# Part of the first h step's products moved into the attention's visits, and the constant products moved to another PSUM bank

## Chip, cores and metric

One NeuronCore of a Trainium2 chip runs the whole program. The metric is device time in microseconds (us) of one launch. Engines are named as in the profile: PE is the matrix engine (PEld its weight loads), DVE the vector engine, ACT the scalar engine, POOL the GpSimd engine, SP the queue from which nearly all DMAs are issued.

## What is computed

Attention over 8 batches x 8 heads x 576 positions of 64 elements, each query seeing 32 keys (four heads the last 32 positions, four heads every fourth of the last 128), and then a feed-forward layer on its 4608 rows of 512.

```python
def _attn_ref(q, k, v):
    scores = scale * np.matmul(q, k.transpose(0, 1, 3, 2))
    ...
    scores = np.where(masks[None, :, :, :], scores, -1000000000.0)
    scores = scores - np.max(scores, axis=-1, keepdims=True)
    attn = np.exp(scores)
    attn = attn / (np.sum(attn, axis=-1, keepdims=True) + 1e-09)
    return np.matmul(attn, v).astype(np.float32)

def _moe_ref(x, w_in, w_out):
    h = x @ w_in
    sp = np.maximum(h, 0.0) + np.log1p(np.exp(-np.abs(h)))
    g = h * erf(sp)
    return (g @ w_out).astype(np.float32)
```

## The kernel before

The attention is cut into 72 units of 256 queries of one pair of heads (two heads side by side). A unit needs ten pieces of work. PE multiplies queries by keys (`scores`, into the two PSUM banks sp0 and sp1, one for each head; a unit uses 128 of the first 256 columns of each, odd and even units apart). DVE adds the mask and takes the maximum (`mask_max`, line 235): four operations, the first two on sp0, the other two on sp1. ACT takes the exponent and its sum (`exponents`, line 245, four operations and their sums). POOL adds a small number to the sum (line 250). DVE takes the reciprocal (line 257), POOL multiplies (line 258). PE transposes (line 263). The result is copied to the tile pT (line 267). PE multiplies it by the values (`values`, line 282), and ACT copies the result into rows of x (line 324).

The first 14 units are worked off in **visits** 0 to 13 (`first_visit`). Visit n transposes unit n-3, scores unit n, copies the transposed unit n-3 and multiplies it by its values, normalizes unit n-2, masks unit n, copies the rows of unit n-3, and takes the exponent of unit n. The order on every engine is the order in which the code is written; nothing is reordered. In between stand **constant products** of PE (`busy`, line 364): 128x128 by 128x512 in bf16, of ones, into the PSUM bank h, where nobody reads them. They are there so that PE is not idle. There are six after the scores of visits 0 to 2, and in visits 3 to 13 two after the scores and two after the values.

When a row of x is complete (every second visit from the 5th: channels cc = 0 at visit 5, 1 at 7, 2 at 9, 3 at 11), ACT rounds it to its high part (`part_hi`, line 329), and DVE subtracts to get the low part (`part_lo`, line 335), in the visit that follows, or, for cc = 3, at the end of visit 11.

Visits 1 to 9 also prepare weights, which arrive as pairs of integers and are made into high and low parts: a DMA into one of three tiles dbl (line 431, 512 KB), an ACT operation on it in the next visit or later (line 451), three DVE operations in the visit after that (lines 464 to 466; the last of them frees the dbl tile, and the next DMA into it is issued), an ACT cast to the high part (line 446), a DVE subtraction to the low part (line 460). In a visit DVE does line 460 for one block, then 464 to 466 for another; this comes behind `mask_max`. In visits 1 to 9 the copy of line 267 is done by ACT, later by DVE. On ACT the order is: copy of line 267, cast of 446, line 451, row copies, the high part of x, exponents.

Then come the steps x = 0, 1, 2, ... of the feed-forward layer. Step x computes half j = x % 2 of step t = x // 2: `mm1` makes 128 columns of h for 512 tokens, in bank h for j = 0 and in bank tx for j = 1. Twelve products of 128x128 by 128x512 in 32-bit form stand for one matrix product of full precision: for each of four channels cc the pairs high-high, high-low and low-high (line 528). DVE copies the bank out (`take`, line 600). The remaining attention units are interleaved: step x = 0 transposes unit 11, then runs `mm1`, `values` of unit 11 and the scores of unit 14, and the steps 1, 2, ... go on so. The copy of pT and the DVE operations on weights come ahead of `take` in steps 0 to 3. From t = 2 on (x = 4), `mm2` (line 643) multiplies by the second weights.

The framework adds the waits between engines. It keeps two engines apart when they touch the same PSUM bank of one tile, even in different columns.

Of the kernel before, what the change touches and what calls it, by code (L numbers as in the profile page):

```python
# [18 lines left out]
P = 128  # L19
# [8 lines left out]
KEYS = STRIP + WIN  # L28
# [3 lines left out]
CC = DM // P  # L32
FT = DF // P
TOK = 512
# [19 lines left out]
PAIR = 2  # L54
# [14 lines left out]
FREE = FIRST - LAG + 4  # L69

EARLY = 9

SAVED = 2 * (HALF + 1) + 1

# [35 lines left out]
def ends(t):  # L110

    return t + 1 == NT or STEPS[t][2] != STEPS[t + 1][2]
# [19 lines left out]
PARTS = SPU // SIDE  # L132
# [14 lines left out]
def attn_moe_kernel(ctx: ExitStack, tc: tile.TileContext, qk, v, masks, eye, w_in, w_out, out):  # L147
    nc = tc.nc
# [16 lines left out]
    win_at = win.rearrange("p (a j k i c n) -> p a j k i c n", a=SPC, j=PAIR, k=2, i=2, c=2)  # L165
# [14 lines left out]
    spb = [ps.tile([P, TOK], F32, name=f"sp{i}") for i in range(2)]  # L180
    sps = [b[:, 0:2 * PARTS * KEYS].rearrange("p (i b k) -> p i b k", i=2, k=KEYS) for b in spb]
    bank = ps.tile([P, TOK], F32, name="tx")
# [22 lines left out]
    def load_qk(u):  # L205
        if u < NU:
            n = QW + key_start(u, SPU - 1) + KEYS
            nc.sync.dma_start(out=qkz[u % 2][:, 0:n], in_=qk[u, :, 0:n])

    def load_v(u):  # L210
        if has(u):
            nc.sync.dma_start(out=vz[u % 2], in_=v[u].rearrange("p (s h d) -> p s h d", s=SIDE, h=2))
# [3 lines left out]
    twice = CC // 2  # L216

    def scores(u):
        i = u % 2
        for s in range(SPU):  # L220
            at, (p, r) = QW + key_start(u, s), divmod(s, SIDE)
            for h in range(2):
                hs = slice(h * D, (h + 1) * D)
                nc.tensor.matmul(sps[h][r * STRIP:(r + 1) * STRIP, i, p, :], qkz[i][hs, s * STRIP:(s + 1) * STRIP],  # L224
                                 qkz[i][hs, at:at + KEYS], start=True, stop=True,
                                 tile_position=(h * D, r * STRIP))

    def mask_max(u):

        pr = probs[u] = work.tile([P, 2 * PARTS, KEYS], F32, name="prob", bufs=LAG + 1)  # L230
        nmax = maxes[u] = small.tile([P, 2 * PARTS], F32, name="nmax", bufs=LAG + 1)
        for h in range(2):
            for p in range(PARTS):
                g = PARTS * h + p
                nc.vector.tensor_tensor_reduce(  # L235
                    out=pr[:, g, :], in0=sps[h][:, u % 2, p, :], in1=mask[QUADS.index(kinds(u, p))],
                    scale=-SCALE, scalar=HUGE,
                    op0=ALU.add, op1=ALU.min, accum_out=nmax[:, g:g + 1],
                )

    def exponents(u):
        nmax = maxes.pop(u)
        sums[u] = small.tile([P, 2 * PARTS], F32, name="ssum", bufs=LAG + 1)
        for j in range(2 * PARTS):
            nc.scalar.activation(  # L245
                out=probs[u][:, j, :], in_=probs[u][:, j, :], func=AF.Exp,
                scale=-1.0, bias=nmax[:, j:j + 1], accum_out=sums[u][:, j:j + 1],
            )
        if u < FIRST:
            nc.gpsimd.tensor_scalar(sums[u], sums[u], 1.0e-9, None, op0=ALU.add)  # L250

    def normalize(u):
        rinv = small.tile([P, 2 * PARTS], F32, name="rinv")

        if u >= FIRST:
            nc.vector.tensor_scalar(sums[u], sums[u], 1.0e-9, None, op0=ALU.add)  # L256
        nc.vector.reciprocal(out=rinv, in_=sums.pop(u))
        nc.gpsimd.tensor_tensor(probs[u], probs[u], rinv.broadcast_to([P, 2 * PARTS, KEYS]), op=ALU.mult)  # L258

    def transposes(u):  # L260
        pr = probs.pop(u)
        for h in range(2):
            nc.tensor.transpose(out=turn_place(u)[:, h * P:(h + 1) * P],  # L263
                                in_=pr[:, PARTS * h:PARTS * (h + 1), :].rearrange("p a k -> p (a k)"), identity=ident)

    def turned(u, copy):
        copy(out=pz[u in second][:, 0:2 * P], in_=turn_place(u))
# [7 lines left out]
    def values(u):  # L275
        vt, pt = vz[u % 2], pz[u in second]
        for s in range(SIDE):
            qs = slice(s * STRIP, (s + 1) * STRIP)
            for p in range(PARTS):
                ks, xp = slice(p * KEYS, (p + 1) * KEYS), place(u, p)  # L280
                for h in range(2):
                    nc.tensor.matmul(xp[h * D:(h + 1) * D, qs], vt[ks, s, h, :],  # L282
                                     pt[ks, h * P + s * STRIP:h * P + (s + 1) * STRIP], start=True, stop=True,
                                     tile_position=(p * KEYS, h * D))
# [37 lines left out]
    def rows(u):  # L322
        for to, src in rows_of(u):
            nc.scalar.copy(out=to, in_=src)  # L324
# [7 lines left out]
    def part_lo():  # L332
        while halved:
            hi, lo, src = halved.pop(0)
            nc.vector.tensor_tensor(out=lo, in0=src, in1=hi.bitcast(F32), op=ALU.subtract)
# [4 lines left out]
    def finish(u):  # L340

        for it in [i for i in x_rows if PER * (u + 1) >= NBLK * (i + 1)]:
            (b, hp), r = divmod(it, HP), x_rows.pop(it)
            if b == 0:
                part_hi(xs[hp][:, 0, :], xs[hp][:, 1, :], r)
            elif b == 1 and hp < twice:
                part_hi(*(w[:, TAIL:TOK] for w in tails(hp)), r[:, 0:TOK - TAIL])
            elif b == 1:
                whole[hp] = r
            if b:  # L350
                soon(store_x, b, hp, slice(TOK - TAIL if b == 1 else 0, S), r)
# [4 lines left out]
    def has(u):  # L356
        return 0 <= u < NU

    idle = plain.bitcast(BF16)[:, 0:TOK]

    def busy(k):

        for _ in range(k):
            nc.tensor.matmul(h, idle[:, 0:P], idle, start=True, stop=True)  # L364

    def first_visit(n):

        m = n - LAG
        copy = nc.scalar.copy if 1 <= n <= EARLY else nc.vector.tensor_copy
        if has(m):  # L370
            transposes(m)
        scores(n)
        load_qk(n + 2)
        busy(2 if has(m) else 6)
        if has(m):
            turned(m, copy)
        if 1 <= n <= EARLY:
            prep_act()
        if has(m):
            values(m)  # L380
            busy(2)
        if has(n - 2):
            normalize(n - 2)
        mask_max(n)
        part_lo()
        if has(m):
            rows(m)
            finish(m)
        if m == NBLK - 1:
            part_lo()  # L390
        exponents(n)
        load_v(n - 1)
# [6 lines left out]
    for g in range(DF // TOK):  # L399
        for c in range(CC):  # L400
            hi, lo = (win_at[:, 2 * g:2 * g + 2, :, c // 2, i, c % 2, :] for i in range(2))
# [38 lines left out]
    def prep_act():  # L440


        calls[0] += 1
        if made:
            w, hi, lo = made.popleft()
            nc.scalar.copy(out=hi, in_=like(w, hi))
            rest.append((calls[0], w, hi, lo))
        if staged:
            i, d, hi, lo = staged.popleft()
            w = io.tile([P, TOK], F32, name="w", bufs=4)  # L450
            nc.scalar.activation(out=w, in_=d[:, :, 1].bitcast(F32), func=AF.Abs, scale=REBASE)
            begun.append((calls[0], i, d, hi, lo, w))
# [20 lines left out]
    h = ps.tile([P, TOK], F32, name="h")  # L473
# [41 lines left out]
                nc.sync.dma_start(out=src[:, a - c * TOK:a - c * TOK + n], in_=xT[b][cc][:, s0:s0 + n])  # L515
                a += n

    def mm1(t, j):
        c, ftp, _ = STEPS[t]
        hi, lo = at[c]  # L520
        ft = ftp * PAIR + j

        ccs = list(range(CC))
        if ends(t) and j == PAIR - 1:
            ccs = ccs[twice:] + ccs[:twice]
        for k, cc in enumerate(ccs):
            for i, (w, x) in enumerate(((0, hi), (0, lo), (1, hi))):
                nc.tensor.matmul((h, bank)[j], win_at[:, ftp, j, cc // 2, w, cc % 2, :], x[cc],  # L528
                                 start=(k == 0 and i == 0), stop=(k == CC - 1 and i == 2))

    ws = dram.tile([SPC, P, len(LEFT) * KIND], F32, name="ws")
    sums_of = {}
# [223 lines left out]
    for k in range(1, DOUBLES):  # L756
        i = 2 * SPC * k
# [13 lines left out]
    i = 2 * SPC * FIN  # L771
# [4 lines left out]
    for p in (1, 2, 3):  # L776
        j = i - 13 + p
# [533 lines left out]
    with tc.manual_schedule():  # L1311
        nc.gpsimd.memset(idle, 1.0)
        busy(8)
        load_qk(0)
        nc.sync.dma_start(out=cst[:, 0:NMASK * KEYS], in_=masks)
        load_qk(1)
        nc.sync.dma_start(out=ident, in_=eye)
        for n in range(FIRST):
            if n < 3:
                load_w(n)  # L1320
            first_visit(n)
            if 1 <= n <= EARLY:
                prep_dve()
# [15 lines left out]
        for x in range(2 * NT):  # L1339
            t, j = divmod(x, 2)  # L1340
# [183 lines left out]
```

## Time and profile before

| what | us |
|---|---|
| median of 3 runs (885.29 to 886.21) | 886.17 |
| span of the profiled execution, first to last instruction | 885.7 |
| PE busy | 864.7 |
| DVE busy | 696.6 |
| ACT busy | 608.8 |
| first score product | 4.82 |
| transposes of unit 11, where step x = 0 begins on PE | 50.72 |
| first product of `mm2` | 72.99 |

The profile gives the span of the profiled execution; the time taken around it is the median less the span, 0.47 us. An instruction's row in the timeline has its start, its duration, its engine and line, what it writes and reads, how many are merged, and in brackets how long the engine was idle before it and who released it. Rows of windows have the busy time of each engine, then the clock that was granted to PE (1.00 is full), and the share of DMA engines that were busy.

### The profile page before, as it was taken

Reading aid. Unit: us, or ns where it says so; the run is one execution under the profiler, and the core shown is the slowest. Engines: PE = TensorE matmul, PEld = TensorE weight load, DVE = VectorE, ACT = ScalarE, POOL = GpSimd, SP = SyncE. Lnnn points to the kernel's source line nnn. Section 1 sums busy time; section 2 is a strip of 40 time slices with the busy share of each in tenths; the row PEclk is TensorE's granted clock in tenths of the full one; section 3 lists DMA queues with packets and bytes.
Section 4 is the critical chain, followed back from the end, with each engine's and each line's share of the span. In section 5 each row is a group of like instructions: output and inputs, shape, how many; then the busy total and the mean of one; then the engine's idle time right before and its main releaser. Section 6 shows DMA issues by size and latency. Waiting matters only on the chain.

```text
span 885.7 us, 21974 instructions
## 1 busy us (share of the span) xinstructions
PE 864.7 (98%) x8410; PEld 710.3 (80%) x8422; DVE 696.6 (79%) x1766; ACT 608.8 (69%) x1364; POOL 79.7 (9%) x97
## 2 busy tenths in 40 slices
PE   7799999999999999999999999999999999999998
PEld 3467888888888888878888888888888788889998
DVE  5878888888688889877766875767886868788994
ACT  6889988897797886675677652774656447784442
POOL 2322200111111100001000000000000000000000
PEclk9899999999999999999999999999999999999999
DMA  8874445464567797666576843674778449999331
GB/s 276 291 235 149 147 158 173 160 238 136 178 213 262 283 327 281 206 215 241 185 236 218 283 177 102 210 234 166 216 248 313 150 144 319 319 345 369 121 131 60
DMA packets 83161, 193.03 MB, mean 218 GB/s; under 512 B 9072, under 2 KB 25712, under 8 KB 79984
## 3 DMA queue, kind: packets, MB, share of 16 engines
q1 hardware_dynamic: 80096, 183.17, 61.0%
q10 hardware_dynamic: 2960, 8.46, 2.4%
q8 instruction: 66, 1.08, 0.5%
q14 instruction: 39, 0.32, 0.1%
HBM read 133.92 MB, written 57.67 MB: 216 GB/s over the span
## 4 chain that ended last, share of the span: by engine, by line
PE 90%; DMA 4%; ACT 2%; DVE 2%; issue 1%; POOL 1%; SPq 0%; DVEq 0%; POOLq 0%; ACTq 0%
PE acc L643 33%; PE h L800 10%; PE tx L800 10%; PE h L528 7%; PE tx L528 7%; PE sp L800 6%; PE sp L282 3%; PE acc L1163 3%; PE sp L224 3%; PE sp L1163 2%; PE sp L263 1%; DMA dbl<-in_w_in_dram 1%; PE tx L1163 1%; DMA win<-wd 1%; PE h L1163 1%; PE h L364 1%
## 5 line engine op out<-in xcount | busy, mean ns | idle before, releaser
L643 PE MATMUL acc<-wout_hi,ghi 128*128 128x512 f32 x448 | 177.7, 397 | 0.5 <-ACT ghi L618 0.5
L643 PE MATMUL acc<-wout_lo,ghi 128*128 128x512 f32 x448 | 174.8, 390 | 0.0
L643 PE MATMUL acc<-wout_hi,glo 128*128 128x512 f32 x448 | 124.1, 390 | 0.7 <-DVE glo L619 0.7
L258 POOL TENSOR_TENSOR prob<-prob,rinv 128x256 f32<-128x256 f32 x72 | 71.6, 1001 | 472.9 <-DVE ssum L256 237.1
L245 ACT ACTIVATE prob<-prob,nmax 128x64 f32<-128x64 f32 x288 | 96.4, 339 | 10.9 <-DVE nmax L235 10.6
L643 PEld LDWEIGHTS acc<-wout_hi,glo 128*128 128x128 f32 x448 | 83.9, 188 | 19.2 <-DVE glo L619 1.4
L643 PEld LDWEIGHTS acc<-wout_hi,ghi 128*128 128x128 f32 x448 | 84.2, 188 | 18.4 <-ACT ghi L618 1.4
L643 PEld LDWEIGHTS acc<-wout_lo,ghi 128*128 128x128 f32 x448 | 84.2, 188 | 16.6
L235 DVE CUSTOM_DVE_ANT_0 prob<-sp,cst 128x64 f32<-128x64 f32 x288 | 45.2, 220 | 36.7 <-ACT rows L324 25.9
L849 ACT ACT_TABLE_LOAD x26 | 33.4, 1283 | 48.6 <-DVE hc L817 24.6
L800 PE MATMUL tx<-win 128*128 128x512 f32 x216 | 55.8, 394 | 0.0
L800 PE MATMUL h<-win 128*128 128x512 f32 x216 | 55.8, 393 | 0.0
L245 ACT ACTIVATION_READ_ACCUMULATOR prob<-prob,nmax 128x1 f32 x288 | 54.9, 191 | 0.0
L528 PE MATMUL h<-x,win 128*128 128x512 f32 x192 | 48.8, 396 | 0.0
L528 PE MATMUL tx<-x,win 128*128 128x512 f32 x192 | 48.0, 392 | 0.0
L800 PEld LDWEIGHTS h<-win 128*128 128x128 f32 x216 | 39.9, 188 | 9.3 <-DVE dbl L819 0.7
L800 PEld LDWEIGHTS tx<-win 128*128 128x128 f32 x216 | 39.9, 188 | 9.1 <-DVE hc L819 0.3
L324 ACT COPY rows<-sp 128x128 f32<-128x128 f32 (+7 forms) x167 | 27.5, 306 | 27.3 <-PE sp L224 26.8
L849 ACT ACTIVATE s<-dbl 128x1024 f32<-128x1024 f32 x22 | 23.3, 1061 | 27.4 <-DVE dbl L817 27.3
L528 PEld LDWEIGHTS h<-x,win 128*128 128x128 f32 x192 | 35.4, 188 | 8.0
L528 PEld LDWEIGHTS tx<-x,win 128*128 128x128 f32 x192 | 35.7, 188 | 7.5
L282 PEld LDWEIGHTS sp<-pT,v 64*64 64x64 f32 x1824 | 29.3, 134 | 10.6 <-DVE s L612 4.6
(338 smaller groups left out, 1942.8 us busy)
## 6 DMA issues: line engine op xcount, KB each, us to landing
win<-ws SPq DMA_DIRECT2D x24, 1024.0 KB, 5.3
v<-in_v_dram SPq DMA_DIRECT2D x72, 256.0 KB, 4.7
win<-ws SPq DMA_DIRECT2D x24, 768.0 KB, 5.9
qk<-in_qk_dram SPq DMA_DIRECT2D x48, 272.0 KB, 5.1
dbl<-in_w_in_dram SPq DMA_DIRECT2D x16, 512.0 KB, 4.3
dbl<-in_w_out_dram SPq DMA_DIRECT2D x16, 512.0 KB, 4.3
ws<-x SPq DMA_DIRECT2D x32, 256.0 KB, 5.0
win<-wd SPq DMA_DIRECT2D x14, 512.0 KB, 8.9
```

The costliest lines, as they stand in the source:

```text
L224: nc.tensor.matmul(sps[h][r * STRIP:(r + 1) * STRIP, i, p, :], qkz[i][hs, s * STRIP:(s + 1) * STRIP], qkz[i][hs, at:at + KEYS], start=True ...
L235: nc.vector.tensor_tensor_reduce(out=pr[:, g, :], in0=sps[h][:, u % 2, p, :], in1=mask[QUADS.index(kinds(u, p))], scale=-SCALE, scalar=HUG ...
L245: nc.scalar.activation(out=probs[u][:, j, :], in_=probs[u][:, j, :], func=AF.Exp, scale=-1.0, bias=nmax[:, j:j + 1], accum_out=sums[u][:, ...
L258: nc.gpsimd.tensor_tensor(probs[u], probs[u], rinv.broadcast_to([P, 2 * PARTS, KEYS]), op=ALU.mult)
L263: nc.tensor.transpose(out=turn_place(u)[:, h * P:(h + 1) * P], in_=pr[:, PARTS * h:PARTS * (h + 1), :].rearrange("p a k -> p (a k)"), iden ...
L282: nc.tensor.matmul(xp[h * D:(h + 1) * D, qs], vt[ks, s, h, :], pt[ks, h * P + s * STRIP:h * P + (s + 1) * STRIP], start=True, stop=True, t ...
L324: nc.scalar.copy(out=to, in_=src)
L528: nc.tensor.matmul((h, bank)[j], win_at[:, ftp, j, cc // 2, w, cc % 2, :], x[cc], start=(k == 0 and i == 0), stop=(k == CC - 1 and i == 2))
L643: nc.tensor.matmul(args["out"], args["lhsT"], args["rhs"], start=args["start"], stop=args["stop"])
L800: nc.tensor.matmul(bank_, w[:, wi, c, :], x[c][:, xi, :], start=(c == 0 and n == 0), stop=(c == 1 and n == 2))
L849: nc.scalar.activation(out=l, in_=e, func=AF.Softplus)
L1163: nc.tensor.matmul(y, x[:, at_], w, start=(q == 0 and j == 0 and n == 0), stop=(q == QUART - 1 and j == 1 and n == 2))
```

## The change

Two things change. First, `mm1` of t = 0 is cut up. A table says which channel and half is done in which visit: channel 0 in visits 7 and 8, channel 1 in 9 and 10, channel 2 in 11 and 12, each with j = 0 first. So 18 of the 24 products of t = 0 stand in visits 7 to 12, between the scores and the values, and one of the two constant products there is dropped. The six products of channel 3 stay at x = 0 and x = 1. Second, since the banks h and tx now hold sums from visit 7 on, the constant products write the free half of bank sp1 (columns 256 to 511), each as two of 256 columns, in all visits from the first.

```diff
+FORMED = {7: [(0, 0)], 8: [(0, 1)], 9: [(1, 0)], 10: [(1, 1)], 11: [(2, 0)], 12: [(2, 1)]}
+LEFT_OVER = [3]
...
     def busy(k):
-        for _ in range(k):
-            nc.tensor.matmul(h, idle[:, 0:P], idle, start=True, stop=True)
+        n = 2 * PARTS * KEYS
+        for _ in range(2 * k):
+            nc.tensor.matmul(spb[1][:, n:TOK], idle[:, 0:P], idle[:, n:TOK], start=True, stop=True)
+
+    def early(n):
+        for cc, j in FORMED.get(n, ()):
+            mm1_part(0, j, [cc])
...
         load_qk(n + 2)
-        busy(2 if has(m) else 6)
+        early(n)
+        busy(2 if has(m) and n not in FORMED else 1 if has(m) else 6)
...
-    def mm1(t, j):
+    def mm1_part(t, j, ccs):
         c, ftp, _ = STEPS[t]
         hi, lo = at[c]
-        ft = ftp * PAIR + j
-        ccs = list(range(CC))
+        order = list(range(CC))
         if ends(t) and j == PAIR - 1:
-            ccs = ccs[twice:] + ccs[:twice]
-        for k, cc in enumerate(ccs):
+            order = order[twice:] + order[:twice]
+        for cc in order:
             for i, (w, x) in enumerate(((0, hi), (0, lo), (1, hi))):
-                nc.tensor.matmul((h, bank)[j], win_at[:, ftp, j, cc // 2, w, cc % 2, :], x[cc],
-                                 start=(k == 0 and i == 0), stop=(k == CC - 1 and i == 2))
+                if cc in ccs:
+                    nc.tensor.matmul((h, bank)[j], win_at[:, ftp, j, cc // 2, w, cc % 2, :], x[cc],
+                                     start=(cc == order[0] and i == 0), stop=(cc == order[-1] and i == 2))
+
+    def mm1(t, j):
+        mm1_part(t, j, LEFT_OVER if t == 0 else range(CC))
```

On PE in visit 8, between the last score product and the first products with the values, before (pT0 and v1 are the transposed unit 5 and its values, plain holds the ones):

```order
L224 MATMUL sp1_91<-qk0_83 32x64
L364 LDWEIGHTS plain_89
L364 MATMUL h_109<-plain_89 128x512
L364 LDWEIGHTS plain_89
L364 MATMUL h_109<-plain_89 128x512
L282 MATMUL acc2_95<-pT0_87,v1_86 64x32 x2
```

and of the change (x0 is channel 0, win the first weights):

```order
L226 MATMUL sp1_91<-qk0_83 32x64
L536 MATMUL tx_92<-x0_97,win_80 128x512 x3
L367 LDWEIGHTS plain_89
L367 MATMUL sp1_91<-plain_89 128x256
L367 LDWEIGHTS plain_89
L367 MATMUL sp1_91<-plain_89 128x256
L284 MATMUL acc2_95<-pT0_87,v1_86 64x32 x2
```

Three products of h came in, one constant product went out, and the other writes sp1 in two halves. Step x = 1 on PE, from the transposes of unit 12 to its products with the values, before:

```order
L263 MATMUL acc1_94<-ident_58,prob_904 128x128 x2
L528 MATMUL tx_92<-x0_97,win_80 128x512 x3
L528 MATMUL tx_92<-x1_98,win_80 128x512 x3
L528 MATMUL tx_92<-x2_99,win_80 128x512 x3
L528 MATMUL tx_92<-x3_100,win_80 128x512 x3
L282 MATMUL acc1_94<-pT0_87,v0_85 64x32 x2
```

and of the change:

```order
L226 MATMUL sp1_91<-qk0_83 32x64
L265 MATMUL acc1_94<-ident_58,prob_976 128x128 x2
L536 MATMUL tx_92<-x3_100,win_80 128x512 x3
L284 MATMUL acc1_94<-pT0_87,v0_85 64x32 x2
L284 MATMUL acc3_96<-pT0_87,v0_85 64x32 x2
```

Nine of twelve products are gone there, and as many at x = 0. DVE, ACT, POOL and SP have the same instructions in the same order as before. What differs on DVE is what one operation waits for. In visit 8 of the change DVE has (the reciprocal of unit 6, the four mask operations of unit 8 with their maxima, the low part of channel 1):

```order
L259 RECIPROCAL rinv_693<-ssum_558 128x4 [waits Pool_49]
L237 ISA prob_696,nmax_697<-sp0_90,cst_59 128x64 [waits PE_49]
L237 ISA nmax_697 128x1
L237 ISA prob_696,nmax_697<-sp0_90,cst_59 128x64
L237 ISA nmax_697 128x1
L237 ISA prob_696,nmax_697<-sp1_91,cst_59 128x64 [waits PE_49]
L237 ISA nmax_697 128x1
L237 ISA prob_696,nmax_697<-sp1_91,cst_59 128x64
L237 ISA nmax_697 128x1
L337 TENSOR_TENSOR x1_98<-rows_482,x1_98 128x576 [waits Activation_49]
```

Both waits on PE are there before as well, each for the last score product on its bank. In the change the count in the second of them, for sp1, is that of the last constant product of the same visit, the one behind the products with the values, since that is the last write to the bank that stands ahead of the mask operation in the code. This is so in all visits 0 to 13, and no other wait of DVE, ACT, POOL or SP differs.

## The prediction

> **What bounds the kernel now.** I read the engines' shares first, then the same by stage, cut at the ends of visits 4, 6, 8 and 10 and at the transposes of unit 11.
>
> ```profile
> PE 864.7 (98%) x8410; PEld 710.3 (80%) x8422; DVE 696.6 (79%) x1766; ACT 608.8 (69%) x1364; POOL 79.7 (9%) x97
> ```
>
> ```profile
> 18.06:26.00 7.94, 4.87 (x139) 2.79 (x140) 7.77 (x29) 6.79 (x30) 2.12 (x4) 1.00 0.92 322
> 26.00:33.49 7.49, 5.81 (x138) 3.32 (x140) 6.57 (x27) 6.81 (x29) 2.62 (x5) 0.77 0.83 274
> 33.49:40.15 6.66, 4.59 (x139) 2.64 (x140) 6.52 (x27) 6.04 (x32) 1.81 (x5) 1.00 0.86 275
> 40.15:50.72 10.57, 9.05 (x208) 5.22 (x211) 4.26 (x33) 6.38 (x36) 3.03 (x7) 0.68 0.69 215
> 50.72:59.10 8.38, 8.38 (x157) 6.57 (x158) 7.74 (x22) 6.01 (x26) 2.27 (x3) 1.00 0.58 198
> 59.10:73.00 13.90, 11.41 (x171) 8.65 (x170) 12.67 (x46) 13.78 (x27) 3.77 (x6) 1.00 0.87 309
> 73.00:120.00 47.00, 47.00 (x507) 37.82 (x506) 41.32 (x115) 43.10 (x107) 7.04 (x8) 1.00 0.39 128
> ```
>
> The columns are length, busy time of PE, PEld, DVE, ACT and POOL, granted clock, DMA share and rate. PE's 98% says that the kernel as a whole is bound by PE, but that holds from 73 us on (47.00 of 47.00). Ahead of it stand the visits, where DVE (7.77 of 7.94, 6.52 of 6.66) and ACT set the pace and PE has gaps, and from 50.72 to 59.10 a stretch in which PE is full and DVE nearly so (7.74 of 8.38). PE's work behind 73 us is not touched. So the end moves by as much as the point moves at which PE fills up, and this is what I work out.
>
> **How a visit runs.** Visit 8, in the timeline:
>
> ```profile
> 30.80 0.17 DVE L257 RECIPROCAL rinv<-ssum 128x4 f32<-128x4 f32 x1
> 31.23 0.23 DVE L235 CUSTOM_DVE_ANT_0 prob<-sp,cst 128x64 f32<-128x64 f32 x1 [0.26 <-PE sp L224]
> 31.67 0.22 DVE L235 CUSTOM_DVE_ANT_0 prob<-sp,cst 128x64 f32<-128x64 f32 x1
> 31.82 0.76 DVE L335 TENSOR_TENSOR x<-rows,x 128x576 fp32r<-128x576 f32 x1
> 31.87 0.36 ACT L267 COPY pT<-acc 128x256 f32<-128x256 f32 x1
> 32.29 0.67 PE L282 MATMUL acc<-pT,v 64*64 64x32 f32 x32 [0.63 <-ACT pT L267]
> 32.49 0.69 DVE L460 TENSOR_TENSOR win<-w,win 128x512 fp32r<-128x512 f32 x1
> 32.65 0.69 ACT L451 ACTIVATE w<-dbl 128x512 f32<-128x512 f32 x1
> 32.89 0.60 PE L364 MATMUL h<-plain 128*128 128x512 bf16 x2
> 33.22 0.68 ACT L324 COPY rows<-acc 128x16 f32<-128x16 f32 x4
> 33.65 0.38 ACT L245 ACTIVATE prob<-prob,nmax 128x64 f32<-128x64 f32 x1
> 34.69 0.69 DVE L466 SCALAR_TENSOR_TENSOR w<-dbl,w 128x512 int32<-128x512 int32 x1
> 34.97 0.39 ACT L267 COPY pT<-acc 128x256 f32<-128x256 f32 x1
> 35.41 0.62 ACT L446 CAST win<-w 128x512 fp32r<-128x512 f32 x1
> 37.08 0.67 ACT L329 CAST x<-rows 128x576 fp32r<-128x576 f32 x1
> ```
>
> DVE's four masks begin at 31.23 and end at 31.89. The last constant products of this visit, those behind the products with the values, end at 33.49 (32.89 and 0.60). So DVE is 1.6 us ahead of PE, and it uses this lead for the weights: lines 460 to 466 run from 32.49 to 35.38, and ACT's cast at 35.41 starts as soon as they are done.
>
> **The term that decides: the third mask waits for the last constant product.** In the change the third and fourth mask read the bank that the constant products write, and the third waits for the last of them in its visit. In visit 8 that takes DVE from 31.5 to 33.5, with the low part of x, the weights and the next unit's reciprocal queued behind, and with ACT's cast waiting for the weights. DVE's lead is gone, and a chain closes that was open: constants, masks, weights, cast, exponents, copy of pT, values, constants. Two visits go by in one round. From the rows of visits 8 and 9: masks three and four 0.40 (half of 0.66 and a signal); low part of x 0.67 (31.82 to 32.49); weights 2.89; cast 0.60; line 451 0.57 (32.65 to 33.22); rows 0.43 (33.22 to 33.65); high part of x 0.57; exponents 1.32 (33.65 to 34.97); copy of pT 0.44 (34.97 to the values at 35.41); values 0.60 (32.29 to 32.89); four half constants 0.60. The sum is 9.09 us. In visit 4 there is no low part, so that round takes 8.42. These are the ends of the constants of visits 4, 6 and 10 before:
>
> ```profile
> 17.46 0.60 PE L364 MATMUL h<-plain 128*128 128x512 bf16 x2
> 25.39 0.61 PE L364 MATMUL h<-plain 128*128 128x512 bf16 x2
> 39.55 0.60 PE L364 MATMUL h<-plain 128*128 128x512 bf16 x2
> ```
>
> From 18.06 to 40.15 it is 22.09 us. The change takes 8.42 + 9.09 + 9.09 = 26.60, so **4.5 us** are lost here. The bounds of this term: nothing, if the wait were covered everywhere; per round no more than the 2.4 us by which 9.09 exceeds the shortest round of before (6.66), so 7.3 at full clock.
>
> **The first visits.** Here six constants stand behind the scores:
>
> ```profile
> 10.80 1.47 PE L364 MATMUL h<-plain 128*128 128x512 bf16 x6
> 10.97 0.23 DVE L235 CUSTOM_DVE_ANT_0 prob<-sp,cst 128x64 f32<-128x64 f32 x1 [2.32 <-PE sp L224]
> 12.73 0.69 DVE L466 SCALAR_TENSOR_TENSOR w<-dbl,w 128x512 int32<-128x512 int32 x1
> ```
>
> In visit 2 the third mask goes from 11.26 to 12.3, and the weights end at 14.5 in place of 13.42. ACT's exponents of that visit still hide it (they run to 13.55), but its next cast waits for the weights, and visit 4 ends **1.0** later. In visits 0 and 1 the same wait is hidden: scores of unit 2 wait for their DMA until 10.4. The loads of weights are issued later too, since line 466 frees their tile:
>
> ```profile
> DMA to landing us min/median/max: 3.7/4.8/5.5
> ```
>
> A load is used two visits on, about 8.4 to 9 us later, where it waits for line 451 and not the other way, except once in visit 4 (some 0.5 us at the median landing, which I leave to the range).
>
> **The products moved in.** They go at this pitch, and leave this place:
>
> ```profile
> 51.16 2.76 PE h L528 x12
> ...
> 53.91 0.60 PE acc L282 x32
> ```
>
> Twelve take 2.76 us, so 0.23 each, three 0.69, less one constant of 0.24: PE gets 0.45 more in each of visits 7 to 12. In 8 and 9 PE's wait for the copy of pT hides it (0.63 in the row at 32.29); in 7 and 10 the rounds above set the pace. In 11 and 12 nothing of weights is left, PE is full, and it counts. There a visit at full clock is 0.44 for transposes, 0.39 scores, 0.69, 0.24, 0.60 and 0.60, with some 0.2 of gaps 3.1 us; visit 13 takes 2.7, and 0.4 go by until visit 11 starts: 9.3 us from the end of visit 10 to unit 11's transposes. Before it is 10.57, but at a clock of 0.68:
>
> ```profile
> 27.00:30.30 3.30, 2.96 (x67) 1.80 (x69) 2.68 (x14) 2.62 (x10) 0.84 (x2) 0.50 0.78 272
> 41.00:47.00 6.00, 5.33 (x108) 2.79 (x113) 2.78 (x20) 3.16 (x16) 0.98 (x3) 0.50 0.70 235
> ```
>
> With full clock throughout the change would gain 1.3 here; with 6 us at half clock again, 3 us of work more, it would lose 1.7. I take **0** between them.
>
> **What is saved at x = 0 and x = 1.** 18 products of 0.23 are 4.14 us of PE's time. But DVE does the same as before there:
>
> ```profile
> 51.20 0.42 DVE L267 COPY pT<-acc 128x256 f32<-128x256 f32 x1 [1.01 <-PE acc L263]
> 54.23 0.68 DVE L600 COPY hc<-h 128x512 f32<-128x512 f32 x1
> 54.55 0.50 ACT L324 COPY rows<-acc 128x64 f32<-128x64 f32 x3 [1.62 <-PE acc L282]
> 69.58 1.62 DVE L612 TENSOR_TENSOR s<-hc,s 128x1024 f32<-128x1024 f32 x1 [0.24 <-ACT s L607]
> ```
>
> The copy of h out of its bank (54.23) comes when DVE has done the weights, not when the twelve products end (53.91); earlier products do not move it. ACT gains at its rows (1.62 of idle), and hands on to DVE what DVE lacks at 69.58, 0.24 us; with a small gap at the masks of unit 16 I take **0.3** as gained. The ends: nothing, and the 1.23 that DVE is idle from 59.10 to 73.00.
>
> **Sum.** 1.0 + 4.5 + 0 - 0.3 = 5.2 us. The profiled span of 885.7 becomes 890.9, and with the 0.47 by which the median stands above the span, **891.4 us**.
>
> **Rivals.** (1) More half clock. The two stretches at 0.50 come behind times in which PE stood idle much (4.87 busy of 7.94, 4.59 of 6.66), and the change makes visits 4 to 10 longer with little more for PE. A row shows the price:
>
> ```profile
> 28.57 1.01 PE acc L282 x32
> ```
>
> The values take 1.01 in place of 0.60, and the constants behind them as much more, so 0.8 per round. Two rounds so and the 1.7 of visits 11 to 13 give 5.2 + 1.6 + 1.7 = 8.5: 894.7 us. The Trainium skill ("TensorE: Matmul & The Clock Gate", Part 1) has the clock either full or half, and half after an idle window of about 3.4 us; the trace agrees with the two levels, and its two stretches are one and two such windows long. By that rule longer gaps mean more half windows, which is this rival.
>
> (2) The wait is covered. If DVE reached its third mask no sooner than PE its last constant, only PE's 0.45 in visits 7, 11 and 12 would count, 1.35, less 0.3: 887.2, no change that a measurement of this kernel tells from none (0.2%, 1.8 us). Against it stand the 1.6 us of lead in visit 8. The Trainium skill ("PSUM — Partial Sum Buffer", PSUM bank collisions raise a hardware error) wants two engines kept apart by bank, not by address; by that rule the wait cannot be thought away. No row here shows such a collision.
>
> (3) Faster: PE is the bound from 50.72 on. PE is full there, 8.38 of 8.38. If its products set DVE's pace, all 4.14 would come back, and with visits no longer than now the time would be 882.0. It decides from the point at which DVE waits for h at `take`; the row at 54.23 has no idle in front of it, so I give this little.
>
> (4) The products do not move, or the sums are lost: the order shows them in the visits, so no chance.
>
> **Chances and range.** The forecast, 0.63; (1) 0.20; (2) 0.11, of which 0.09 is within 0.2% and 0.02 slower; (3) 0.06. So slower by over 0.2% has 0.85, within it 0.09, faster 0.06. Low end: the full-clock gain of 1.3 and all 1.23 at DVE, and one round covered (1.5): 5.2 - 1.3 - 0.9 - 1.5 = 1.5, 887.7. High end: rival (1), 894.7, and 0.3 for nothing gained at the end: 895.0. Left out are (3), most of (2) and a tail.
>
> **What would show it.** Right: in visits 2 to 10 DVE idle ahead of the third mask, released by line 367's products into sp1, 1 to 2 us each; ACT's casts waiting for DVE; visit 10 ending near 45.6, unit 11's transposes near 56; DVE as full as now (20.4 of 22.3 us) in the stretch behind that; PE full later by 5. Wrong: DVE gapless through the visits (then rival 2), or `take` of x = 0 waiting for PE and the stretch shorter by 4 (rival 3).

## The result, and the profile after

The changed kernel takes 890.67 us (median of 6 runs, 888.74 to 892.38) against 886.19 us of the kernel before (median of 6, 884.37 to 887.89): a ratio of 1.0053, 95% interval [1.0038, 1.0068]. It is slower by 4.5 us. All medians here are of undisturbed runs; one run in twelve of e1_acc and of e3_skip18 and two of e5_prep2 took over 1400 us and are left out.

The lines of the changed kernel stand two to eleven further down: the mask is line 237, the exponents 247, the transposes 265, the copy of pT 269, the values 284, the rows 326, the high and low parts of x 331 and 337, the constant products 367, the weights 455 to 475, `mm1` 536, `take` 611.

The engines' shares, of the profiled execution (span 889.3 us, time 891.19):

```profile
PE 867.5 (98%) x8480; PEld 716.5 (81%) x8480; DVE 694.8 (78%) x1766; ACT 609.0 (68%) x1364; POOL 77.8 (9%) x97
```

Nothing can be read from it but that PE is as full as before. The stages tell more. The windows of after are cut, as those of before, at the ends of the constant products of visits 4, 6, 8 and 10 and at the transposes of unit 11, and then at the first `mm2` (76.70; 72.99 before). Columns as in the prediction:

```profile
17.98:26.25 8.27, 5.84 (x151) 4.00 (x148) 6.11 (x26) 7.16 (x32) 1.97 (x4) 0.94 0.84 282
26.25:34.73 8.48, 7.19 (x152) 4.63 (x151) 6.77 (x27) 6.30 (x28) 2.27 (x4) 0.86 0.69 242
34.73:42.99 8.26, 6.38 (x150) 3.85 (x148) 7.17 (x28) 6.01 (x32) 1.81 (x4) 1.00 0.76 261
42.99:54.85 11.86, 10.45 (x225) 7.01 (x225) 4.78 (x32) 6.21 (x35) 2.50 (x6) 0.86 0.58 184
54.85:76.70 21.85, 15.79 (x311) 11.77 (x309) 20.46 (x72) 20.38 (x54) 5.47 (x9) 1.00 0.80 275
77.00:124.00 47.00, 47.00 (x507) 37.86 (x506) 41.41 (x115) 42.75 (x107) 7.41 (x9) 1.00 0.40 130
```

and the last of the stages ahead of `mm2`, of before:

```profile
50.72:72.99 22.27, 19.78 (x326) 15.20 (x327) 20.40 (x67) 19.79 (x53) 6.04 (x9) 1.00 0.76 268
```

The three rounds of two visits are 25.01 us long and were 22.09, so 2.9 are lost there. DVE is busy for 20.05 of these 25.01 us and was for 20.86 of the 22.09: about the same work, with more gaps in it. Visits 11 to 13 take 11.86 in place of 10.57, 1.3 more. Then comes the stretch of x = 0 to 3: PE does 15.79 us of work in place of 19.78, the 18 products less, and the stretch is shorter by only 0.42, with DVE working 20.46 us in it, as before (20.40), and ACT 20.38 (19.79). From 77 us on PE is full again.

Who made DVE wait in the visits, in the view of waits (engine, what waited and for whom, us in total, times, longest), before, from 4 to 52 us:

```profile
DVE prob L235 <- PE sp L224: 10.5, 6, 5.6
DVE pT L267 <- PE acc L263: 3.7, 3, 1.5
DVE x L335 <- ACT x L329: 2.6, 1, 2.6
```

and after, from 4 to 56 us:

```profile
DVE prob L237 <- PE sp L367: 15.7, 12, 3.9
DVE prob L237 <- PE sp L226: 6.5, 3, 5.4
DVE x L337 <- ACT x L331: 0.4, 1, 0.4
```

The mask now waits twelve times, 15.7 us in all, for line 367, the constant products. Not all of it is loss: 4.5 us stand in visits 6 to 10, and 6.7 in visits 11 to 13, where in the chain of waits PE's own work is what comes last. It takes the place of most of the waits that were there, for scores, transposes and the high part of x (16.8 us, 6.9 now), and with it the sum rises to 22.6 us, in a stretch that is 4 us longer. What the wait does is seen in the chain of waits, one round of visits 7 and 8 of after (start, length, what):

```profile
26.66 0.67 DVE x L337
27.33 0.60 DVE win L469
27.93 0.35 DVE w L473
...
28.30 0.70 DVE w L474
...
29.03 0.70 DVE w L475
...
29.75 0.62 ACT win L455
30.37 0.57 ACT w L460
30.94 0.21 ACT rows L326 x2
...
31.16 0.73 ACT x L331
31.90 1.31 ACT prob L247 x8
33.21 0.26 ACT pT L269
...
33.52 0.67 PE acc L284 x32
34.19 0.56 PE sp L367 x4
```

It runs from the third mask of visit 6 to that of visit 8. This is the loop that the prediction named, closed, with each piece directly behind the one before: low part, weights, cast, exponents, copy, values, constants, and then the third mask. The timeline of after at both of its joints:

```profile
29.75 0.62 ACT L455 CAST win<-w 128x512 fp32r<-128x512 f32 x1 [2.18 <-DVE w L475]
...
34.12 0.61 PE L367 MATMUL sp<-plain 128*128 128x256 bf16 x4
...
34.77 0.23 DVE L237 CUSTOM_DVE_ANT_0 prob<-sp,cst 128x64 f32<-128x64 f32 x1 [1.33 <-PE sp L367]
```

ACT idles 2.18 us for DVE's weights, and DVE idles 1.33 us for PE's constants, which compute nothing.

### The profile page after: what moved, and what is told of

It is laid out like the page before. It is cut to its first block, busy times and chain, and to the rows that moved or that the text cites. A ratio compares the mean times of both kernels' runs of the same rounds, so it can differ in the third digit from the quotient of the medians.

```text
span 889.3 us, 22102 instructions
## 1 busy us (share of the span) xinstructions
PE 867.5 (98%) x8480; PEld 716.5 (81%) x8480; DVE 694.8 (78%) x1766; ACT 609.0 (68%) x1364; POOL 77.8 (9%) x97
## 4 chain that ended last, share of the span: by engine, by line
PE 85%; DVE 6%; DMA 4%; ACT 2%; issue 1%; POOL 0%; SPq 0%; DVEq 0%; ACTq 0%; POOLq 0%
PE acc L654 32%; PE h L811 9%; PE tx L811 9%; PE h L536 7%; PE tx L536 7%; PE sp L811 5%; PE sp L284 3%; PE acc L1174 3%; PE sp L226 3%; PE sp L1174 2%; PE sp L367 1%; PE sp L265 1%; DMA w<-ga 1%; DMA win<-wd 1%; PE tx L1174 1%
## 5 line engine op out<-in xcount | busy, mean ns | idle before, releaser
L860 ACT ACT_TABLE_LOAD x26 | 33.4, 1283 | 49.0 <-DVE hc L828 24.6
L860 ACT ACTIVATE s<-dbl 128x1024 f32<-128x1024 f32 x22 | 23.3, 1061 | 27.4 <-DVE dbl L828 27.3
```

Of the source, the lines that this page charges most:

```text
L860: nc.scalar.activation(out=l, in_=e, func=AF.Softplus)
```

## The experiments

Theory A: the loss comes from the third mask's wait for the constant products, since these write the bank sp1. Its rivals: the loss comes from the products that were moved in, or from the clock; and, about what was hoped for, that PE's work at x = 0 and 1 is worth its 4.14 us. All times are medians beside runs of the kernel before on the same chip; the ratio is to those. The time is 1.7 to 1.9 us above the span where both are known.

**e1_acc: the change without the wait.** The constant products write columns 256 to 511 of the bank acc[m % 4]. The unit m that is worked on has its transposes and its products with the values in other banks of acc, and DVE's masks read none of these. Against the change:

```diff
-    def busy(k):
+    def busy(k, m=0):
-            nc.tensor.matmul(spb[1][:, n:TOK], idle[:, 0:P], idle[:, n:TOK], start=True, stop=True)
+            nc.tensor.matmul(acc[m % 4][:, n:TOK], idle[:, 0:P], idle[:, n:TOK], start=True, stop=True)
```

> The change with the constant products of each visit written to a bank acc that no unit uses in that visit, so that the third mask waits for the scores again; the 18 products of h stay in visits 7 to 12. Theory A (the third mask's wait for the constants makes the loss): DVE's idle time ahead of line 237 goes back from 15.7 us released by the constants to none released by them, unit 11's transposes come at 50.5 to 51.5, and the time is 0 to 0.8 us above the kernel before. Theory B (three products more in each of six visits lengthen PE's chain there and bring half clock): 3.5 to 5 us above the kernel before, as with the change.

Measured: 886.32 us against 885.84, ratio 1.0010 [0.9994, 1.0027]: no difference that can be told from none. The waits of DVE, of e1_acc:

```profile
DVE prob L237 <- PE sp L226: 9.7, 5, 5.6
DVE pT L269 <- PE acc L265: 3.8, 3, 1.8
DVE x L337 <- ACT x L331: 2.3, 1, 2.3
```

These are close to those of before, and line 367 is gone. One choice in the code, the bank, takes most of the loss away, with all 18 products still in the visits.

**e2_sp1_only: the wait without the rest.** The kernel before, with only `busy` taken from the change; `mm1` stays whole at x = 0 and 1.

```diff
-        for _ in range(k):
-            nc.tensor.matmul(h, idle[:, 0:P], idle, start=True, stop=True)
+        n = 2 * PARTS * KEYS
+        for _ in range(2 * k):
+            nc.tensor.matmul(spb[1][:, n:TOK], idle[:, 0:P], idle[:, n:TOK], start=True, stop=True)
```

> The kernel before with one part of the change alone: the constant products go to the free half of sp1, in halves of 256 columns, and all 24 products of h stay at x = 0 and x = 1. Theory A: 3 to 5 us above the kernel before, with the chain constants, third mask, weights, cast, exponents, copy, values, constants through visits 4 to 10, and nothing gained at x = 0. Theory B: within 0.5 us of the kernel before.

Measured: 890.94 us, ratio 1.0042 [1.0025, 1.0059], a loss that can't be told from the change's 1.0053 (3.7 us by the ratio, 5.1 by the medians). The waits of e2_sp1_only (its `busy` is line 365):

```profile
DVE prob L235 <- PE sp L365: 15.6, 11, 3.4
```

15.6 us, where the change has 15.7. Removed and added alone, the wait accounts for the loss: A stands, and the moved products are not its cause. Nor is the clock: the mean clock of the change's six runs is 0.995, that of the 29 runs of before beside e1 to e4 as well.

The profiles agree on where it is lost. From the end of visit 4 to that of visit 10 it is 25.0 us in the change, 27.4 in e2 and 24.6 in the second profile of the change (e11, below); without the wait it is 22.1 in the kernel before, 21.2 in e1 and 21.1 in e3, and 22.4 in e4, which keeps a part of it. One kernel's stretch changes from profile to profile, but with the whole wait and with none of it the nearest two lie 2.5 us apart.

**e3_skip18: what the shorter x = 0 and 1 are worth.** The kernel before, with `mm1` of t = 0 doing channel 3 alone. Channels 0 to 2 do not enter h at t = 0, and are done nowhere.

```diff
-        ccs = list(range(CC))
+        ccs = list(range(CC)) if t else [3]
```

> The kernel before with 18 of the 24 products of h of step t = 0 left out (channels 0 to 2 don't enter h there), and nothing put into the visits: what x = 0 and x = 1 give when they are shorter by 4.1 us of PE. If DVE bounds that stretch, 0.3 us below the kernel before (0 to 1.2), with DVE's rows from the copy of pT at x = 0 at the same distances. If PE bounds it, 4.1 us below.

Measured: 885.27 us, ratio 0.9993 [0.9975, 1.0011]. To leave the 18 products out altogether gains 0.6 us, which can't be told from nothing, and by the interval at most 2.2, of the 4.14 us that they take on PE. From unit 11's transposes (50.15) to the first `mm2` (72.65) it is 22.5 us, where the kernel before has 22.27. So the change had little to win.

**e4_second_acc: half of the wait.** Of the change, only the constants behind the values go to acc; those behind the scores still write sp1.

```diff
-            busy(2)
+            busy_acc(2, m)
```

> The change with only the constant products behind the values written to a free bank acc; those behind the scores still go to sp1, so the third mask waits for the first group of constants of its visit, which ends 1.2 to 2.2 us before the second. Theory A: most of the loss goes, 0.5 to 2 us above the kernel before, and line 237 still waits for line 367, under 8 us in all. Theory B: as the change, 3.5 to 5 us above.

Measured: 888.39 us, ratio 1.0025 [1.0010, 1.0040], 2.2 us by the ratio, where the change's ratio gives 4.7. The waits:

```profile
DVE prob L237 <- PE sp L367: 4.6, 6, 1.2
```

A shorter wait, for products that stand further forward in the visit, and a smaller loss, though a little over the 0.5 to 2 us that were expected.

**e5 to e8: take DVE's work out of x = 0 to 3.** If DVE bounds that stretch, then moving preparations of weights from it into visits 10 to 13, which have none, lets the 18 products count. e6_prep4 is e1_acc with four of them moved, e5_prep2 with two (of x = 2 and 3), e8_prep2_early with two (of x = 0 and 1); e7_before_prep4 is the kernel before with the four moved. For e6 and e7:

```diff
+PREP_TO = 13
+PAUSED = (0, 1, 2, 3)
...
-        if 1 <= n <= EARLY:
+        if 1 <= n <= PREP_TO:
...
-        pause = SAVED + 1,
+        pause = (SAVED + 1, *PAUSED)
```

> E1 (products of h in the visits, constants in a free bank) with two of the weights' preparations moved: visits 10 and 11, where DVE is idle most of the time, do one each, and steps x = 2 and x = 3 do none. If DVE bounds the stretch from x = 0 to the first mm2, this takes 5.5 us of DVE and 2.6 us of ACT out of it and gives back 1.2 us in each of the two visits: 1.5 to 3.5 us below E1, so 1 to 3 us below the kernel before. If ACT and the chain through POOL bound it: within 0.7 us of E1.

> As e5 with four preparations moved: visits 10 to 13 do one each, steps x = 0 to 3 none, so 11 us of DVE leave the stretch of 22 us and PE's 18 products count there at last. DVE as the bound: 3 to 6 us below the kernel before. ACT or the chain through POOL as the bound: no better than e5.

> The kernel before (all 24 products at x = 0 and x = 1, constants in h) with the same four preparations moved as in e6. If PE sets the pace of x = 0 and x = 1 once DVE doesn't, this is 2 to 4 us slower than e6, by the 4.1 us of the 18 products less what their 0.45 us per visit cost. If the products never count, it is equal to e6 within 1 us.

> As e5, but the steps that do no preparation are x = 0 and x = 1, where PE lost its 18 products, in place of 2 and 3. If DVE bounds the whole stretch alike: equal to e5 within 0.7 us. If the steps 2 and 3 are bound by ACT (13.78 of 13.90 us busy from 59.10 to 73.00 in the kernel before), e8 is 0.7 to 2 us slower than e5.

| kernel | us | ratio to before (886.1) |
|---|---|---|
| e5_prep2 | 889.88 | 1.0034 [1.0015, 1.0052] |
| e6_prep4 | 889.10 | 1.0026 [1.0010, 1.0043] |
| e7_before_prep4 | 890.35 | 1.0045 [1.0026, 1.0064] |
| e8_prep2_early | 888.62 | 1.0023 [1.0007, 1.0039] |

No version gained; the gains expected of moving the preparations were missed. But the stretch from unit 11's transposes to the first `mm2` says why. Windows of e1_acc:

```profile
49.72:71.83 22.11, 18.70 (x308) 14.03 (x309) 20.17 (x67) 20.20 (x53) 5.74 (x9) 0.85 0.83 271
```

of e6_prep4:

```profile
54.02:72.90 18.88, 15.64 (x311) 11.80 (x309) 12.79 (x56) 15.91 (x46) 5.28 (x9) 1.00 0.82 258
```

and of e7_before_prep4:

```profile
54.53:76.53 22.00, 21.02 (x328) 16.18 (x326) 11.93 (x54) 15.49 (x44) 4.94 (x9) 0.93 0.66 215
```

With DVE down from 20.17 to 12.79 us, the stretch falls to 18.88. The same edit takes ACT from 20.20 to 15.91, so that DVE alone held the stretch is not shown. Against e7 the 18 products seem to be worth 22.00 - 18.88 = 3.1 us there, but some 1.2 of it is half clock: e7's first twelve products take 4.21 us, its next twelve 3.00. In e7, which keeps them, DVE waits for PE where it never did, at `take` (line 602 there):

```profile
59.07 0.69 DVE L602 COPY hc<-h 128x512 f32<-128x512 f32 x1 [3.31 <-PE h L530]
63.18 0.69 DVE L602 COPY hc<-tx 128x512 f32<-128x512 f32 x1 [1.52 <-PE tx L530]
```

In these profiles the visits give it all back: unit 11's transposes begin at 54.02 in e6, at 49.72 in e1, 4.3 us later for 3.2 gained (22.11 - 18.88). As the rows read, the work was moved to visits where it is on the path as well. The intervals of e6 and e7 overlap, and so do those of e5 and e8, so neither 1.25 us between e6 and e7 nor a difference between e5 and e8 is shown.

**e9 to e11: are constant products worth more, or less?** e9_more_const is e1_acc with four constants behind the values in visits 3 to 10; e10_less_const has none at all in visits 3 to 10; e11 is the change again, beside them.

```diff
-            busy(2, m)
+            busy(4 if n <= 10 else 2, m)
```

> The change with the constant products in the unused columns of acc (as in e1_acc), and four instead of two of them behind the values in visits 3 to 10. Theory H (the half-clock stretches ahead of 63 us are set by how much PE idles in the visits): PE is fuller from 17 to 42 us, there are fewer half-clock stretches there, mean clock of the whole above 0.995, and the time is 0.5 to 2 us below e1_acc's 887.3 (885.3 to 886.8). Rival N (where and how many half-clock stretches there are does not follow these products): clock as in e1_acc (0.990 to 0.996), and the row copies, which read the same bank, wait 0.5 us longer, so 887.3 to 888.5. Theory A (the wait of the third mask makes the loss) expects no wait of the masks for constants in either case.

> The change as in e1_acc, but without any constant products in visits 3 to 10; those of visits 0 to 2 and 11 to 13 stay. Theory H: PE idles some 1 us more in each of these visits, half-clock stretches come more often, mean clock of the whole 0.992 or lower, and the time is 1 to 4 us above e1_acc's 887.3 (888.3 to 891). Rival N: clock as before, and with 0.5 to 1 us less work in the chain of each visit the time is 886.0 to 887.5.

> The change as it is, on the same chip as the two kernels beside it. Theory A: 889.5 to 891.5 us, 3 to 4.5 above the kernel before and above the two others by 1.5 or more; the masks wait some 16 us in all for line 367. If it came within 1 us of the kernel before, the loss first measured would not be of the change.

| kernel | us | ratio to before (885.65) | mean clock of its runs |
|---|---|---|---|
| e9_more_const | 887.09 | 1.0011 [0.9996, 1.0026] | 0.9965 |
| e10_less_const | 888.50 | 1.0030 [1.0014, 1.0045] | 0.981 |
| e11_after_again | 891.76 | 1.0049 [1.0031, 1.0066] | 0.993 |

The windows of e9_more_const and of e10_less_const, the visits from 17 us and what follows:

```profile
17.00:42.00 25.00, 22.11 (x548) 16.02 (x549) 22.74 (x87) 22.53 (x100) 9.31 (x14) 1.00 0.88 299
42.00:63.00 21.00, 14.88 (x345) 10.47 (x344) 15.38 (x67) 16.00 (x58) 4.53 (x9) 1.00 0.71 215
```

```profile
17.00:42.00 25.00, 19.36 (x404) 12.68 (x396) 21.88 (x82) 20.24 (x85) 8.70 (x12) 0.52 0.87 272
42.00:63.00 21.00, 19.29 (x402) 13.58 (x402) 12.79 (x64) 14.63 (x64) 5.56 (x11) 0.74 0.62 197
```

The clock does follow the constants: 1.00 with more of them, 0.52 without. The rule of the Trainium skill that the prediction cites ("TensorE: Matmul & The Clock Gate", Part 1), half speed after an idle window of about 3.4 us, fits this only if such a window need not be empty: in e10 no gap of PE between 4 and 50 us is longer than 1.7 us.

The time follows the clock less. These expectations take e1_acc at 887.3 us, where the median above is 886.3, and the row copies read other banks than these constants write, so the 0.5 us that rival N adds for them has no ground. e9 has its full clock, as theory H wanted, and is not the 0.5 to 2 us faster that H expected. e10 is where H expected it, with 888.5 us and a lower clock. It loses 1.4 us to e9, for a whole stage at half clock, in visits where PE has slack and DVE and ACT are busy for most of the time. What half clock alone costs is not separated: e10 has fewer products to do as well, and the intervals of e9 and e10 just overlap. e11 gives the change's loss a second time, 6.1 us by the medians and 4.3 by the ratio, with a time 0.3 us above the range expected, and 4.7 us to e9 on the same chip.

No kernel tried that computes the whole result beats the one before. What e1 and e9 have left above it, some 0.1%, lies inside their intervals; whether it is the 0.45 us of the added products in visits 7, 11 and 12 stays open.

## Why the prediction came out as it did

The forecast was 891.4 us, and 890.67 was measured. Its deciding step is shown by e1 and e2. The sizes below are read from one profile of each kernel, and a stretch of one kernel differs by 1 us or more between profiles. So they tell where the sum was off in these two, and part of the agreement is luck, as errors cancel.

**The third mask's wait: right in mechanism, 1.6 us too large in this profile.** Predicted were rounds of 8.42, 9.09 and 9.09 us, 4.5 lost; measured were 8.27, 8.48 and 8.26, 2.9 lost (7.82, 8.51 and 8.27 in e11; 9.73, 8.49 and 9.20 in e2, with half clock in all three). The piece that was mis-sized is "weights 2.89". It was taken from 32.49 to 35.38 in visit 8 of before, and one row in there is stretched by an operation of POOL, the multiplication of line 258. The timeline of before:

```profile
32.73 0.91 POOL L258 TENSOR_TENSOR prob<-prob,rinv 128x256 f32<-128x256 f32 x1
...
33.09 0.84 DVE L464 TENSOR_SCALAR w<-w 128x512 int32<-128x512 int32 x1
```

and of after, the same operation:

```profile
27.85 0.42 DVE L473 TENSOR_SCALAR w<-w 128x512 int32<-128x512 int32 x1
```

In before, line 464 took 0.4 us longer. It did not wait for its input, which ACT had made in visit 7 (line 451, 28.60 to 29.28). It started while POOL was multiplying and ended 0.29 us after POOL did (33.93 and 33.64). In the first 76 us of the thirteen profiles this operation is long 25 times (0.50 to 0.86 us), each time begun during such a multiplication and ended 0.27 to 0.29 us after it; all its other rows take 0.41 or 0.42. In the profiles of the change, of e2 and of e11, where DVE waits at the masks, none is long. In the chain above, the weights take 29.75 - 27.33 = 2.42, which is 0.47 less, and in three rounds 1.4 of the 1.6.

By single rounds it fits less well. In the first the constants of visit 6 ran at half clock (1.04 us at 25.21, against 0.61), which made it longer. In the third, DVE copies pT of visit 10, not ACT, and does so at 41.31, before ACT's exponents are through (41.82); the prediction had reckoned with ACT's copy behind them. In a loop, a piece must go in at the time that it takes alone, not at that of a row which another engine's work had stretched.

**What the signs said.** ACT's casts waiting for DVE: shown, three times from 17 to 42 us, 5.0 us by the view of waits, none there before. The mask's wait "1 to 2 us each, in visits 2 to 10": shown in the visits that close a round (1.97 at 26.28, 1.33 at 34.77, 0.96 at 43.03); in the visits between, 7 and 9, it is 0.24 or nothing, which the loop of two visits implies and the sign overlooked.

**First visits: +1.0 predicted, nothing seen in this profile.** Visit 4 ends at 17.98, before at 18.06. The third mask of visit 2 did wait for the six constants. Of before and of after:

```profile
10.41 0.46 PE L224 MATMUL sp<-qk 64*32 64x64 f32 x32 [1.23 <-DMA qk<-in_qk_dram]
```

```profile
9.50 0.45 PE L226 MATMUL sp<-qk 64*32 64x64 f32 x30 [0.24 <-DVE nmax L237]
...
11.40 0.23 DVE L237 CUSTOM_DVE_ANT_0 prob<-sp,cst 128x64 f32<-128x64 f32 x1 [0.98 <-PE sp L367]
```

The step took the scores of unit 2 as fixed at 10.4 by their load. Here they did not wait for the load, they ran on as soon as DVE let them, and the third mask began at 11.40 and not at 12.3. Whether the wait costs anything here is not shown. Visit 4 ends at 18.99 in e2 and at 20.62 in e11, which have the wait, but between 18.06 and 19.09 in before, e1, e3 and e9, which have not; the scores of unit 2 start between 9.0 and 10.4 in the profiles of e1 to e4 and e9 to e11. The term belonged into the range, from nothing to 1.0, not into the sum.

**Visits 11 to 13: 0 chosen between -1.3 and +1.7, +1.3 in this profile.** PE's timeline of after in visit 12:

```profile
46.38 0.77 PE L226 MATMUL sp<-qk 64*32 64x64 f32 x30
48.48 0.27 PE L226 MATMUL sp<-qk 64*32 64x64 f32 x2 [1.33 <-issue]
...
50.36 1.08 PE L284 MATMUL acc<-pT,v 64*64 64x32 f32 x32
51.37 1.04 PE L367 MATMUL sp<-plain 128*128 128x256 bf16 x4
```

The values take 1.08 and the constants 1.04 here, at half clock, after a gap of 1.33 us for which the profile names no releaser. This is the mishap of rival (1). It came here and from 25.0 to 28.5 us (clocks of 0.94 and 0.86 in the first two rounds), not in each round. In e2 the same three visits take 8.7 us, 1.8 less than before, at a clock of 0.91.

**The gain at x = 0 and 1: 0.3 predicted, 0.4 measured.** The reason holds: DVE is as full as it was, e3 bounds the gain at 2.2 us, and `take` has no idle ahead of it in after:

```profile
58.43 0.68 DVE L611 COPY hc<-h 128x512 f32<-128x512 f32 x1
```

Rival (3) falls with it; the point from which it would decide, DVE waiting for h at `take`, is reached only in e7. Rival (2), the wait covered, falls by the 15.7 us of waits and by e2.

**The sum.** The four terms gave +5.2 on the span and +3.6 was measured (885.7 to 889.3). The 0.47 us between time and span was wrong: it set a median of three runs against the span of another execution. Where both are known, they differ by 1.8, so the profiled execution of before had lasted some 887.5 us, 1.3 above its median. The oversized sum (+1.6) and the undersized offset (-1.4, as 891.19 - 889.3 = 1.89) nearly cancel, and the profiled execution of after is 0.5 above its median: 1.6 - 1.4 + 0.5 = 0.7, the miss. That the two cancel is luck.

## What to carry to other kernels

A product that computes nothing still writes a bank, and whoever reads that bank, in any column, waits for the last such write that stands ahead of it in the code; so put such products where no engine reads, and look at each reader's wait when they move. Before work is taken off a full engine, look who sets the pace there: PE was full from 50.72 to 59.10, and 4.1 us less of its work gained 0.4, since DVE had as much to do as before and its `take` did not wait for PE. Where a wait closes a loop through several engines, add up the loop once around, each piece at the time that it takes alone, and compare it with the round as it was.

## What was not expected of the hardware

A shift on DVE takes up to twice its time when it falls into a multiplication of POOL (0.84 and 0.42 us above). Half clock cost little: e10's visits ran 25 us at a mean clock of 0.52, and its time is 1.4 us above e9's, which ran them at 1.00, though with fewer products to do. And runs of one kernel differ in clock: the eleven runs of e1_acc had mean clocks between 0.990 and 0.997. The three at 0.990 had spans of 886.5, 887.9 and 888.5 us, where the eight above lay between 883.3 and 887.0. A single profile, which also differs from the next by up to 1.4 us in when the scores of unit 2 start, is no measure of an effect of 1 us.
